# Attention and token mixer on one core: the max tiles in front of the loop made in pairs, with one VectorE maximum over two PSUM banks

## The chip, the cores and the metric

One Trainium2 chip, one of its cores. The metric is the device time of one execution in microseconds (us), less is better. Time before: 1671.52 us, median of 3 runs (1671.33 to 1672.03).

## What is computed

The output mixes two branches row by row with a gate, g = sigmoid(x . gate_w):

```python
q = (x @ wq) in 32 heads of 20;  k = x @ wk;  v = x @ wv      # one k and v for all heads
a = softmax(q k^T / sqrt(20)) v, heads joined, @ wo           # 2048 tokens x 2048 tokens, 32 times
u = gelu(layernorm(x)^T @ w1 + b1)                            # token axis: 640 x 1728
b = (u @ w2 + b2)^T                                           # 640 x 2048, turned back
out = g * a + (1 - g) * b                                     # 2048 x 640, float32
```

x is 2048 x 640. The softmax needs the maximum of every row of scores. The kernel makes it with scores of its own: a max matmul (the rows of q as weights, 512 columns of k as moving data) fills one PSUM bank, 128 queries by 512 keys, and VectorE reduces it to one column of 128 maxima. Four such columns, one for each block of 512 keys, belong to one row of scores.

## The kernel before, in words

The order of the work on each engine is written out by hand: every engine runs its instructions in the order in which the program issues them, and semaphores follow from which tiles they read and write. PSUM has 8 banks of 128 x 512 float32 here.

**Front (to 96.4 us).** x is turned and projected to q, k and v, q goes to a DRAM scratch (q_scr), LayerNorm fills h_hi and h_lo (x normalized, split into a high and a low part for float32 precision).

**The stage in front of the loop (96.4 to 168.2 us, lines 565 to 601).** It makes the first PRO = 8 of the 2 x 14 tiles of u. For each tile fc there are 16 steps (4 quarters hf by 4 chunks c); a step is six matmuls, three products (wh by h_hi, wh by h_lo, wl by h_hi), each on the two row halves of the array at once, into one PSUM bank per half (pu, psb: 2 x 2 banks). So there are 128 steps. Into them the program weaves two other things:

- *Leads* (lead, lines 569 to 572): max work for the loop, done ahead. After some steps, LEAD = 48 times in all, evenly spread from step 3 to step 122, a lead takes one max step of each row half b (ms_next, lines 467 to 487): one max matmul into one of the three banks of ps_m and one VectorE maximum over it (L482) into a column of mtiles. The two matmuls of a lead run on the two halves of the array.
- *Gelu steps* (gelu, lines 515 to 558): when a tile fc is done, ScalarE copies the first bank with the bias, and the further operations on VectorE, ScalarE and GpSimd (add, square, cube, tanh, product, high, low) are put on a list, one of which (or an empty place, None) is taken after each of the next steps (pop_chain). VectorE has two of them: add (L525), which reads the second bank, and cube (L529), which needs ScalarE's square of what add made.

ScalarE and GpSimd also split the next chunks of w1 into wh and wl (w1_upto). When 32 max steps of each half are done, ms_done reduces mtiles to the row maxima of unit 0 of 32 (L493), and store_max and fetch_max bring them to where the loop's score matmuls read them.

**The loop (from 168.2 us).** 326 turns; each weaves score matmuls (L657), exponentials (L660), products with v (L684), further max steps (L479, L482), and the products of the mixer's other tiles and of the output. Its max tiles alternate between ps_m and ps_s. The order of the max steps of a unit is given by ms_next's count k: the key block kq is the slowest, then the pair pr of heads, then the query block qt.

Banks in the stage: ps_m 3, ps_g 1 (used from the loop on), psb 4. Behind the stage psb is given up and ps_s (3) and ps_o (1) take its banks.

Of the kernel before, what the change touches and what calls it, by code (L numbers as in the profile page):

```python
# [9 lines left out]
F32 = mybir.dt.float32  # L10
F32R = mybir.dt.float32r
AF = mybir.ActivationFunctionType
ALU = mybir.AluOpType
AX = mybir.AxisListType
PSUM = bass.MemoryType.PSUM
DRAM = bass.MemoryType.DRAM

P = 128
# [6 lines left out]
NB = 512  # L25
NQB = S // NB
NQ = H // 4
NU = NQB * NQ
PRO = 8
LEAD = 48  # L30
# [9 lines left out]
def mix_kernel(ctx: ExitStack, tc: tile.TileContext, A_x, A_wq, A_wk, A_wv, A_wo,  # L40
               B_x, B_w1, B_b1, B_w2, B_b2, gate_w, out):
    nc = tc.nc
    x = A_x[0]
    y_out = out[0]

    def f32(ap):
        return ap.bitcast(F32)
# [11 lines left out]
    kst = const.tile([P, S], F32R, name="kst")  # L59
# [18 lines left out]
    right = ExitStack()  # L78
# [55 lines left out]
    def load_q(n, name):  # L134
        t = qp.tile([P, 2, NB], F32R, name=name)
        qb, g = divmod(n, NQ)
        cols = slice(qb * NB, (qb + 1) * NB)

        def part(b, j, src):
            o = 64 * b + DH * j  # L140
            rows = q_scr[src, g * 4 * DH:(g + 1) * 4 * DH, cols]
            nc.sync.dma_start(out=f32(t[o:o + DH]), in_=rows.rearrange("(a b d) q -> b d a q", a=2, b=2)[b])

        parts = [lambda b=b, j=j, src=src: part(b, j, src) for b in range(2) for j, src in enumerate((0, 1, 0))]
        if one_by_one[0]:
            q_parts_due.extend(parts)
        else:
            for f in parts:
                f()
        return t  # L150

    qtiles, qmax = {}, {}
    one_by_one, q_parts_due = [False], []

    def new_q(n):
        if n < NU:
            qtiles[n] = load_q(n, "qst")

    def new_qmax(n):
        if n < NU and n not in qmax:  # L160
            qmax[n] = load_q(n, "qmx")
# [285 lines left out]
    u_lo = [view(t, UC * HD2, UC) for t in (u0, slot[0])]  # L447
    pp_pool = ctx.enter_context(tc.tile_pool(name="pp", bufs=11))
    ev = ctx.enter_context(tc.tile_pool(name="ev", bufs=1))
    ps_m = ctx.enter_context(tc.tile_pool(name="ps_m", bufs=3, space=PSUM))  # L450
    ps_g = ctx.enter_context(tc.tile_pool(name="ps_g", bufs=1, space=PSUM))
    mpool = ctx.enter_context(tc.tile_pool(name="mpool", bufs=2))
    mmpool = ctx.enter_context(tc.tile_pool(name="mmpool", bufs=2))

# [1 line left out]
    mtiles = {}  # L456
    ring = []

    def next_bank():
        if not ring:  # L460
            return ps_m.tile([P, NB], F32, name="ms")
        ring[0] ^= 1
        return ps_m.tile([P, NB], F32, name="ms") if ring[0] else ps_s.tile([P, NB], F32, name="s")
    given = [0, 0]
    issued = [0, 0]

    def ms_next(b):
        k = given[b]
        if k >= 32 * NU:
            return None  # L470
        given[b] += 1
        n, r = divmod(k, 32)
        (kq, pr), qt = divmod(r // 4, 2), r % 4

        def step():
            if n not in mtiles:
                mtiles[n] = mpool.tile([P, 16, 4], F32, name="mp")
            ms = next_bank()
            nc.tensor.matmul(ms, qmax[n][64 * b:64 * b + 60, pr, qt * P:(qt + 1) * P],  # L479
                             kst[64 * b:64 * b + 60, kq * NB:(kq + 1) * NB], start=True, stop=True)  # L480
            c = (2 * b + pr) * 4 + qt
            nc.vector.tensor_reduce(mtiles[n][:, c, kq:kq + 1], ms, axis=AX.X, op=ALU.max)  # L482
            issued[b] += 1
            if min(issued) == 32 * n + 1:
                new_qmax(n + 1)

        return step

    def ms_done():
        n = len(row_max)  # L490
        if n < NU and min(issued) >= 32 * (n + 1):
            mm = mmpool.tile([P, 16], F32, name="mm")
            nc.vector.tensor_reduce(mm, mtiles.pop(n), axis=AX.X, op=ALU.max)  # L493
            mn = mmpool.tile([P, 2, 16], F32R, name="mn")
            nc.gpsimd.tensor_scalar(mm, mm, -1.0, None, op0=ALU.mult)
            nc.gpsimd.tensor_copy(mn[:, 0, :], mm)
            nc.gpsimd.tensor_sub(mn[:, 1, :], mm, f32(mn[:, 0, :]))
            row_max[n] = mn
# [14 lines left out]
    chain = []  # L513

    def gelu(d, fc, accs):
        both = fin.tile([P, D], F32, name="yo")
        xg, t1 = both[:, :HD2], both[:, HD2:]
        hi, lo = u_hi[d][:, fc, :], u_lo[d][:, fc, :]
        nc.scalar.activation(xg, accs[0][:, :HD2], AF.Identity, bias=bias[:, NS + fc:NS + fc + 1])

        def square():
            nc.scalar.activation(t1, xg, AF.Square)

        def add():
            nc.vector.tensor_add(xg, xg, accs[1][:, :HD2])  # L525
            square()

        def cube():
            nc.vector.scalar_tensor_tensor(t1, t1, 1.0 / 0.044715, xg, op0=ALU.add, op1=ALU.mult)  # L529

        def tanh():
            nc.scalar.activation(t1, t1, AF.Tanh, scale=GC * 0.044715)

        def high():
            nc.scalar.activation(hi, t1, AF.Copy)

        def low():
            nc.gpsimd.tensor_sub(lo, t1, f32(hi))

        def cube_p():  # L540
            nc.gpsimd.tensor_scalar(t1, t1, 1.0, 1.0 / 0.044715, op0=ALU.mult, op1=ALU.add)
            nc.gpsimd.tensor_mul(t1, t1, xg)

        def prod_p():
            nc.gpsimd.tensor_scalar(t1, t1, 1.0, 1.0, op0=ALU.mult, op1=ALU.add)
            nc.gpsimd.tensor_mul(t1, t1, xg)

        def high_p():
            nc.gpsimd.tensor_copy(hi, t1)
            nc.gpsimd.tensor_sub(lo, t1, f32(hi))  # L550

        if len(accs) == 2 and fc == PRO - 1:
            add()
            chain.extend((cube_p, None, tanh, prod_p, high_p))
        elif len(accs) == 2:
            chain.extend((None, None, add, None, cube, tanh, None, prod_p, None, None, None, high, None, low))
        else:
            chain.extend((square, cube_p, None, tanh, prod_p, high_p))

# [2 lines left out]
        if f:  # L562
            f()

    with tc.tile_pool(name="psb", bufs=2, space=PSUM, side="right") as psb:
        at, skip, last = 0, 3, NS * PRO - 6
        one_by_one[0] = True

        def lead():
            for b in range(2):  # L570
                ms_next(b)()
            ms_done()

        for fc in range(PRO):
            pu = [psb.tile([P, NB], F32, name=f"pu{r}") for r in range(2)]
            for hf in range(4):
                w1_upto(4 * fc + hf + 4)
                for f in [q_parts_due.pop(0) for _ in range(min(len(q_parts_due), 1 + fc // 5))] if fc else []:
                    f()
                wh, wl = w1t.pop(4 * fc + hf)  # L580
                for c in range(HS):
                    st = hf * HS + c
                    for k, (w, h) in enumerate(((wh, h_hi[0]), (wh, h_lo[0]), (wl, h_hi[0]))):
                        for r in range(2):
                            rows = slice(64 * r, 64 * r + 64)
                            nc.tensor.matmul(pu[r][:, :HD2], w[rows, c, :], h[rows, st, :],  # L586
                                             start=(st == 0 and k == 0), stop=(st == NS - 1 and k == 2))
                    done = [max(0, min(x, last) - skip) * LEAD // (last - skip) for x in (at, at + 1)]
                    if done[1] > done[0]:
                        lead()  # L590
                    at += 1
                    pop_chain()
                if fc == 1 and hf == 0:
                    new_q(0)
                if fc == PRO - 2 and hf == 2:
                    assert not q_parts_due
                    one_by_one[0] = False
                    fetch_max(0)
            gelu(0, fc, pu)
            if fc == PRO - 3:  # L600
                store_max(0)

    ps_s = ctx.enter_context(tc.tile_pool(name="ps_s", bufs=3, space=PSUM))
    ps_o = ctx.enter_context(tc.tile_pool(name="ps_o", bufs=1, space=PSUM))

# [26 lines left out]
    last = {"half": None, "ins": None, "sig": None}  # L632
# [331 lines left out]
    for st in range(NS):  # L964
        job = b2_jobs(st)
        if st < FIVE:
            for d in range(2):
                at = len(ph)
                ph += job[d]
        else:  # L970
            at = len(ph) + 6
# [87 lines left out]
    for k in range(len(ph)):  # L1059
        n = 0 if k == 0 else 1 + k % 2  # L1060
# [11 lines left out]
    for n in BLOCKS:  # L1072
# [3 lines left out]
        i = 0  # L1076
        while any(sc[b] < ends[b] for b in range(2)):
            b = int(sc[1] < sc[0])
# [6 lines left out]
        at = [0.0, 0.0]  # L1085
        while any(lanes) or any(fs):
            b = 0 if at[0] <= at[1] and (lanes[0] or fs[0]) or not (lanes[1] or fs[1]) else 1
# [18 lines left out]
    for c in range(CUT // P, DC):  # L1106
        r = min(P, HEAD - c * P)
        for st in held:
            oT, _ = room(len(jobs) - 4 + st - (NS - 4))
            for d in range(2):  # L1110
# [3 lines left out]
                for k, (j, w) in enumerate(((0, wo_hi), (1, wo_hi), (0, wo_lo))):  # L1114
                    nc.tensor.matmul(accs[st, d][:, :HD2], oT[:r, j, c, :], w[:r, c, d * HD2:(d + 1) * HD2],
                                     start=(k == 0 and c == CUT // P), stop=False)
# [5 lines left out]
    for i in range(4):  # L1122
        st = NS - 4 + i
        for d in range(2):
            at = pp_pool.tile([P, NB], F32, name="p")
# [3 lines left out]
            for k, (o, w) in enumerate(((oh, w_last[0]), (ol, w_last[0]), (oh, w_last[1]))):  # L1129
                nc.tensor.matmul(acc[:, :HD2], o[:, i * P:(i + 1) * P], w[:, sl],  # L1130
                                 start=(k == 0 and (st, d) not in accs), stop=(k == 2))
# [32 lines left out]
```

## Time and profile before

| | before |
|---|---|
| median of 3 runs | 1671.52 us |
| the profiled execution: device time | 1671.47 us |
| the profiled execution: span of its instructions | 1669.7 us |
| stage in front of the loop | 96.4 to 168.2 us, 71.8 us |
| TensorE / VectorE / ScalarE / GpSimd busy in the stage | 70.1 / 67.1 / 29.1 / 57.2 us |

How to read it: the span runs from the first instruction's start to the last one's end, and the device time has 1.8 us more around it. PE is TensorE's matmul, PEld its weight load (it runs beside the matmul before), DVE is VectorE, ACT ScalarE, POOL GpSimd, SP SyncE. L482 is line 482 of the kernel. A row of a group of instructions has line, engine, operation, output<-inputs, shapes and xcount, then the busy time in us and the mean of one in ns, then the engine's idle time just before them and who ended it. A row of waits names who waited for whom, in us, with the number of times and the longest. A row of the order of time has start, length, engine, line and operation; instructions of one kind behind each other are merged into one row with their count, and its length runs from the first start to the last end. A row of windows has the busy time of each engine in a stretch with the number of instructions, the clock granted to TensorE (1.00 is full), the DMA share and GB/s. Matmul ends are modelled.

### The profile page before, as it was taken

How to read it: one execution, taken by the hardware profiler on the slowest of the kernel's cores; microseconds unless marked ns; L12 is line 12 of the kernel's file. 1: busy time of each engine (PE TensorE's matmuls, PEld its weight loads, DVE VectorE, ACT ScalarE, POOL GpSimd, SP SyncE). 2: the span in 40 equal slices, each digit the busy share in tenths (PEclk: the TensorE clock that was granted, in tenths of full speed). 3: DMA queues.
4: the chain of work that ended last, by engine and by line, in shares of the span. 5: the costliest groups of instructions: out<-in, count | busy, mean ns of one | idle time of the engine just before them, and what ended most of it. 6: DMA issues, size and time to landing. Idle time of an engine off the chain costs nothing.

```text
span 1669.7 us, 38827 instructions
## 1 busy us (share of the span) xinstructions
PE 1661.0 (99%) x14865; PEld 1105.5 (66%) x14865; DVE 1435.7 (86%) x2732; ACT 1188.0 (71%) x2346; POOL 606.3 (36%) x759
## 2 busy tenths in 40 slices
PE   9999999999999999999999999999999999999998
PEld 7899666666666666666666666666666566666665
DVE  6689899999989999988888988988888998988933
ACT  4434777777777777777777777777777777777775
POOL 6578555455455554422232332122122220111210
PEclk9999999999999999999999999999999999999999
DMA  7665222222132232222222222212222121333611
GB/s 211 205 176 137 79 71 69 78 58 78 53 84 73 71 82 74 58 60 62 66 75 74 55 62 66 61 52 71 63 66 60 55 65 41 96 111 113 189 51 39
DMA packets 178305, 138.20 MB, mean 83 GB/s; under 512 B 33306, under 2 KB 144055, under 8 KB 178119
## 3 DMA queue, kind: packets, MB, share of 16 engines
q1 hardware_dynamic: 177830, 135.39, 28.9%
q8 instruction: 117, 1.92, 0.5%
q14 instruction: 70, 0.57, 0.1%
q10 hardware_dynamic: 288, 0.33, 0.1%
HBM read 102.36 MB, written 31.65 MB: 80 GB/s over the span
## 4 chain that ended last, share of the span: by engine, by line
PE 95%; issue 2%; DVE 1%; SPq 1%; ACT 0%; DMA 0%; POOL 0%; POOLq 0%; DVEq 0%; ACTq 0%
PE o L684 28%; PE ms L479 18%; PE s L657 13%; PE g L750 10%; PE g L929 7%; PE ms L657 5%; PE pp L298 4%; PE s L479 3%; PE pu L586 3%; PE g L875 2%; DVE mp L482 1%; PE ms L831 0%; ACT p L660 0%; PE pt L290 0%; SPq L195 0%
## 5 line engine op out<-in xcount | busy, mean ns | idle before, releaser
L482 DVE TENSOR_REDUCE mp<-ms 128x1 f32<-128x512 f32 x1514 | 967.2, 685 | 130.2 <-PE ms L479 102.7
L660 ACT ACTIVATE p<-s 128x512 f32<-128x512 f32 x1512 | 820.6, 606 | 299.4 <-PE s L657 280.2
L479 PE MATMUL ms<-kst,qmx 60*128 60x512 f32 x1514 | 646.5, 433 | 1.7 <-DVE mp L482 1.7
L657 PE MATMUL s<-qst,kst 62*128 62x512 f32 x1512 | 601.6, 403 | 0.0
L684 PE MATMUL o<-p,v_sb 128*32 128x512 f32 x4096 | 511.3, 601 | 0.0
L479 PEld LDWEIGHTS ms<-kst,qmx 60*128 60x128 f32 x1514 | 279.0, 184 | 244.9 <-ACT p L660 114.7
L482 DVE TENSOR_REDUCE mp<-s 128x1 f32<-128x512 f32 x534 | 355.6, 683 | 12.0 <-PE s L479 11.8
L660 ACT ACTIVATE p<-ms 128x512 f32<-128x512 f32 x536 | 305.1, 599 | 56.8 <-PE ms L657 50.2
L657 PEld LDWEIGHTS s<-qst,kst 62*128 62x128 f32 x1512 | 278.5, 186 | 55.2 <-DVE flag L670 31.0
L929 PE MATMUL g<-slot,wh 64*128 64x320 f32 x1280 | 297.5, 311 | 0.0
L129 POOL TENSOR_TENSOR wl<-wr,wh 128x512 fp32r<-128x512 f32 x176 | 228.6, 1300 | 43.8 <-PE g L750 17.3
L479 PE MATMUL s<-kst,qmx 60*128 60x512 f32 x534 | 230.8, 441 | 0.4 <-DVE yo L525 0.4
L684 PEld LDWEIGHTS o<-p,v_sb 128*32 128x32 f32 x4096 | 97.5, 108 | 185.3 <-issue 177.2
L657 PE MATMUL ms<-qst,kst 62*128 62x512 f32 x536 | 216.8, 405 | 0.0
L929 PEld LDWEIGHTS g<-slot,wh 64*128 64x128 f32 x1280 | 211.6, 184 | 2.0 <-issue 1.7
L750 PE MATMUL g<-slot,wh 64*128 64x320 f32 x864 | 202.1, 313 | 0.1
L750 PE MATMUL g<-u,wh 64*128 64x320 f32 x864 | 201.7, 312 | 0.0
L929 PE MATMUL g<-slot,wl 64*128 64x320 f32 x640 | 199.6, 312 | 0.0
L706 POOL TENSOR_TENSOR ot<-ot,rl 128x512 f32<-128x512 f32 x30 | 31.6, 1052 | 346.6 <-DVE rl L705 346.6
L128 POOL CAST wh<-wr 128x512 fp32r<-128x512 f32 x144 | 88.3, 613 | 188.0 <-PE g L750 81.5
L750 PEld LDWEIGHTS g<-slot,wh 64*128 64x128 f32 x864 | 143.5, 184 | 4.9 <-ACT yo L758 4.0
L750 PEld LDWEIGHTS g<-u,wh 64*128 64x128 f32 x864 | 143.5, 184 | 1.1 <-issue 1.1
(202 smaller groups left out, 2092.8 us busy)
## 6 DMA issues: line engine op xcount, KB each, us to landing
wr<-in_B_w_dram SPq DMA_DIRECT2D x152, 256.0 KB
qmx<-q_scr SPq DMA_DIRECT2D x192, 80.0 KB
qst<-q_scr SPq DMA_DIRECT2D x192, 80.0 KB
slot<-o_scr SPq DMA_DIRECT2D x20, 320.0 KB
y_scr<-yo SPq DMA_DIRECT2D x16, 320.0 KB
o_scr<-oh SPq DMA_DIRECT2D x124, 40.0 KB
o_scr<-ol SPq DMA_DIRECT2D x124, 40.0 KB
q_scr<-qh SPq DMA_DIRECT2D x19, 256.0 KB
```

The source lines that it names most:

```text
L128: nc.gpsimd.tensor_copy(wh, wr)
L129: nc.gpsimd.tensor_sub(wl, wr, f32(wh))
L298: nc.tensor.matmul(pp, w, t, start=first and n == 0, stop=not more and n == len(steps) - 1)
L479: nc.tensor.matmul(ms, qmax[n][64 * b:64 * b + 60, pr, qt * P:(qt + 1) * P], kst[64 * b:64 * b + 60, kq * NB:(kq + 1) * NB], start=True, s ...
L482: nc.vector.tensor_reduce(mtiles[n][:, c, kq:kq + 1], ms, axis=AX.X, op=ALU.max)
L586: nc.tensor.matmul(pu[r][:, :HD2], w[rows, c, :], h[rows, st, :], start=(st == 0 and k == 0), stop=(st == NS - 1 and k == 2))
L657: nc.tensor.matmul(s, kst[64 * b:64 * b + 62, kb * P:(kb + 1) * P], q[64 * b:64 * b + 62, pr, :], start=True, stop=True)
L660: nc.scalar.activation(p, s, AF.Exp, scale=SCALE)
L684: nc.tensor.matmul(o[32 * hh:32 * hh + 32, :], v_sb[:, kb, :], ptiles.pop((u, hh)), start=(kb == 0), stop=(kb == NS - 1), skip_group_check ...
L750: other_tile(half, nc.tensor.matmul(hold["p"][:, :HD2], w[r, fc % HS, :], u[d][r, fc, :], start=(hold["n"] == 1), stop=(hold["n"] == 6 * F ...
L875: other_tile(half, nc.tensor.matmul(hold["p"][:, :HD2], o[r, c, :], w[r, c, d * HD2:(d + 1) * HD2], start=(hold["n"] == 1), stop=(hold["n" ...
L929: other_tile(half, nc.tensor.matmul(hold["p"][:, :HD2], w[r, st % HS, :], h[d][r, st, :], start=(hold["n"] == 1), stop=(hold["n"] == 6 * NS)))
```

## The change

A lead in the stage now takes two max steps of each row half: four max matmuls into two double tiles (m2, two banks each, one for each half), in the order half 0, half 1, half 0, half 1, and then one VectorE maximum for each half over 2 x 512 columns, which writes two neighbouring columns of mtiles. There are 24 leads where there were 48, so the number of max matmuls in the stage stays 96, and that of maxima goes from 96 to 48. The two matmuls of a double tile have the same queries and the key blocks kq and kq + 1; so the count k is taken apart in another order, in the loop too: the lowest bit of kq is now the fastest. The pool of double tiles (psl, 2 x 2 banks) lives only in the stage; ps_m and ps_g are made behind it. In the list of gelu steps, cube, tanh and the product move back by one place each, and high and low stay where they were. The loop keeps its single banks and its maxima over 512.

```diff
-    ps_m = ctx.enter_context(tc.tile_pool(name="ps_m", bufs=3, space=PSUM))
-    ps_g = ctx.enter_context(tc.tile_pool(name="ps_g", bufs=1, space=PSUM))
...
     def next_bank():
-        if not ring:
-            return ps_m.tile([P, NB], F32, name="ms")
...
+    def ms_at(b):
+        k = given[b]
+        n, r = divmod(k, 32)
+        if n not in mtiles:
+            mtiles[n] = mpool.tile([P, 16, 4], F32, name="mp")
+        kq, pr, qt = 2 * (r // 16) + r % 2, r // 8 % 2, r // 2 % 4
+        return n, kq, pr, qt, (2 * b + pr) * 4 + qt
+
+    def ms_mm(ms, b, n, kq, pr, qt):
+        nc.tensor.matmul(ms, qmax[n][64 * b:64 * b + 60, pr, qt * P:(qt + 1) * P],
+                         kst[64 * b:64 * b + 60, kq * NB:(kq + 1) * NB], start=True, stop=True)
+
+    def ms_count(b, n, c):
+        issued[b] += c
+        if min(issued) > 32 * n:
+            new_qmax(n + 1)
...
-        (kq, pr), qt = divmod(r // 4, 2), r % 4
...
-            chain.extend((None, None, add, None, cube, tanh, None, prod_p, None, None, None, high, None, low))
+            chain.extend((None, None, add, None, None, cube, tanh, None, prod_p, None, None, high, None, low))
...
-    with tc.tile_pool(name="psb", bufs=2, space=PSUM, side="right") as psb:
+    with tc.tile_pool(name="psl", bufs=2, space=PSUM) as psl, \
+            tc.tile_pool(name="psb", bufs=2, space=PSUM, side="right") as psb:
...
         def lead():
-            for b in range(2):
-                ms_next(b)()
+            ats = [ms_at(b) for b in range(2)]
+            two = [psl.tile([P, 2, NB], F32, name="m2") for _ in range(2)]
+            for i in range(2):
+                for b, (n, kq, pr, qt, _) in enumerate(ats):
+                    ms_mm(two[b][:, i], b, n, kq + i, pr, qt)
+            for b, (n, kq, _, _, c) in enumerate(ats):
+                given[b] += 2
+                nc.vector.tensor_reduce(mtiles[n][:, c, kq:kq + 2], two[b], axis=AX.X, op=ALU.max)
+                ms_count(b, n, 2)
             ms_done()
...
-                    done = [max(0, min(x, last) - skip) * LEAD // (last - skip) for x in (at, at + 1)]
+                    done = [max(0, min(x, last) - skip) * (LEAD // 2) // (last - skip) for x in (at, at + 1)]
...
+    ps_m = ctx.enter_context(tc.tile_pool(name="ps_m", bufs=3, space=PSUM))
+    ps_g = ctx.enter_context(tc.tile_pool(name="ps_g", bufs=1, space=PSUM))
     ps_s = ctx.enter_context(tc.tile_pool(name="ps_s", bufs=3, space=PSUM))
```

More of the change, by code (lines that the diff above doesn't have):

```diff
@@ L465, in mix_kernel @@
     issued = [0, 0]
+    def ms_at(b):
[12 more added lines that the diff above has]
+            new_qmax(n + 1)
     def ms_next(b):
-        k = given[b]
-        if k >= 32 * NU:
+        if given[b] >= 32 * NU:
             return None
+        at = ms_at(b)
         given[b] += 1
-        n, r = divmod(k, 32)
-        (kq, pr), qt = divmod(r // 4, 2), r % 4
         def step():
-            if n not in mtiles:
-                mtiles[n] = mpool.tile([P, 16, 4], F32, name="mp")
+            n, kq, pr, qt, c = at
             ms = next_bank()
-            nc.tensor.matmul(ms, qmax[n][64 * b:64 * b + 60, pr, qt * P:(qt + 1) * P],
-                             kst[64 * b:64 * b + 60, kq * NB:(kq + 1) * NB], start=True, stop=True)
-            c = (2 * b + pr) * 4 + qt
+            ms_mm(ms, b, n, kq, pr, qt)
             nc.vector.tensor_reduce(mtiles[n][:, c, kq:kq + 1], ms, axis=AX.X, op=ALU.max)
-            issued[b] += 1
-            if min(issued) == 32 * n + 1:
-                new_qmax(n + 1)
+            ms_count(b, n, 1)
         return step
```

## The prediction

> **What bounds the kernel now.** I read the page first, then the busy times by stage, then the waits of TensorE, then VectorE's groups and the order of time inside the one stage that is edited. TensorE is the bound of the whole, and of the edited stage too, but there VectorE is close behind:
>
> ```profile
> span 1669.7 us, 38827 instructions
> PE 1661.0 (99%) x14865; PEld 1105.5 (66%) x14865; DVE 1435.7 (86%) x2732; ACT 1188.0 (71%) x2346; POOL 606.3 (36%) x759
> ```
>
> ```profile
> core 0: us, PE busy (x) PEld busy (x) DVE busy (x) ACT busy (x) POOL busy (x), PEclk, DMA share, GB/s
> ...
> 96.40:168.20 71.80, 70.08 (x866) 67.76 (x866) 67.10 (x119) 29.12 (x57) 57.19 (x58) 1.00 0.56 155
> 168.20:400.00 231.80, 231.39 (x2126) 151.29 (x2124) 207.88 (x394) 176.37 (x351) 118.93 (x155) 1.00 0.28 72
> ```
>
> The stage in front of the loop is the row 96.40 to 168.20: TensorE 70.1 and VectorE 67.1 of 71.8 us, at full clock. Behind it TensorE is busy 231.39 of 231.80 us, and from 168.3 us to the end its waits on other engines are these:
>
> ```profile
> PE s L479 <- DVE yo L525: 0.4, 1, 0.4
> PE g L831 <- DVE row L838: 0.2, 1, 0.2
> ```
>
> So nothing behind the stage can swallow a later start: what the stage loses or gains, the total loses or gains, one for one. Inside the stage, the max matmuls (L479) are the only TensorE work that waited, always for the maximum (L482):
>
> ```profile
> its engine sat idle before it (us, times) until:
>   DVE mp L482: 4.8, 9
> ```
>
> That view adds the weight loads to the matmuls, so 4.8 is not TensorE time; it says who is waited for. VectorE's work in the stage:
>
> ```profile
> L482 DVE TENSOR_REDUCE mp<-ms 128x1 f32<-128x512 f32 x96 | 59.7, 680 | 2.8 <-PE ms L479 1.8 <-PE pu L586 0.3
> L529 DVE SCALAR_TENSOR_TENSOR yo<-yo 128x320 f32<-128x320 f32 x7 | 3.6, 521 | 0.5 <-ACT yo L522 0.5
> ...
> L493 DVE TENSOR_REDUCE mm<-mp 128x16 f32<-128x64 f32 x1 | 0.2, 219 | 0.0
> ```
>
> **How fast TensorE could go.** From the order of time, TensorE only (start, length):
>
> ```profile
> 96.45 0.42 PE L586 MATMUL pu<-slot,wh 64*128 64x320 f32 x2
> ...
> 98.62 0.31 PE L586 MATMUL pu<-slot,wl 64*128 64x320 f32 x2
> ...
> 99.06 0.31 PE L586 MATMUL pu<-slot,wl 64*128 64x320 f32 x2
> 99.20 0.39 PE L479 MATMUL ms<-kst,qmx 60*128 60x512 f32 x2
> 99.44 0.46 PE L586 MATMUL pu<-slot,wh 64*128 64x320 f32 x4
> ...
> 150.26 0.39 PE L479 MATMUL ms<-kst,qmx 60*128 60x512 f32 x1
> ...
> 152.94 0.40 PE L479 MATMUL ms<-kst,qmx 60*128 60x512 f32 x1
> ...
> 168.23 0.30 PE L929 MATMUL g<-slot,wh 64*128 64x320 f32 x1
> ```
>
> A step (six matmuls, three pairs on the two row halves) holds one pair with wl: 98.62 to 99.06, so 0.44 us. A pair of max matmuls costs 99.44 - 99.20 = 0.24. From 150.26 to 152.94 there are two old leads and five steps without a wait: 2.68 us, which is just what a new lead (two pairs) and its five steps hold. The stage runs from 96.45 to the loop's first product at 168.23: 71.78 us.
>
> The new leads come after steps 8, 13, ..., 122: 23 gaps, 22 of five steps, one of four. With no wait at all the stage would take 99.20 - 96.45 + 2 x 0.44 = 3.63 up to the first lead, 22 x 2.68 + 2.24 = 61.20 between leads, and 2 x 0.24 + 6 x 0.44 = 3.12 from the last lead to the end: 67.95, **3.83 less** than now. That is the most that can be won.
>
> **The new wait.** Before, 48 leads of two banks ran round three banks, so a max matmul needed the maximum of three tiles earlier. Now a lead takes both double tiles, so that each tile is asked for again one lead later. TensorE's queue is in order: first matmul of half 0, first of half 1, second of half 0, second of half 1. The first of half 1 waits for half 1's maximum, the last thing VectorE does for the previous lead; the second of half 0 stands behind it, and without that one VectorE cannot start the next pair at all. That closes a ring, priced with these rows:
>
> ```profile
> 99.64 0.69 DVE L482 TENSOR_REDUCE mp<-ms 128x1 f32<-128x512 f32 x1 [0.92 <-PE ms L479]
> ...
> 109.38 6.30 DVE L482 TENSOR_REDUCE mp<-ms 128x1 f32<-128x512 f32 x10
> ...
> 153.91 0.68 DVE L482 TENSOR_REDUCE mp<-ms 128x1 f32<-128x512 f32 x1
> ```
>
> ```profile
> 154.65 0.49 PE L479 MATMUL ms<-kst,qmx 60*128 60x512 f32 x1 [0.20 <-DVE mp L482]
> 154.65 0.64 PE L586 MATMUL pu<-slot,wh 64*128 64x320 f32 x3
> ```
>
> - A max matmul that was waited for takes 0.49 instead of 0.39, and the next one on the other half starts with it (both rows say 154.65). I give 0.49 to the second of half 0.
> - From the end of that matmul to the maximum: 99.20 + 0.39 = 99.59 to 99.64, 0.05.
> - The maximum over 1024 is in no row. Length: 680 ns for 512 and 219 for 64 make 1.03 ns an element, and the 64 were in 16 groups, so groups are not dear; 0.68 + 0.53 = 1.21. Start to start, ten of 512 in 6.30 make (6.30 - 0.68) / 9 = 0.62, so the next starts 0.06 before the end: 1.21 - 0.06 = 1.15. Bounds: below, 1.05 for each (1024 elements with no fixed part); above, two maxima of now, 1.24 start to start and 1.30 long. I take 1.15 and 1.21, since the slope comes from the same instruction.
> - From its end to the waiting matmul: 153.91 + 0.68 = 154.59 to 154.65, 0.06.
>
> Ring: 0.49 + 0.05 + 1.15 + 1.21 + 0.06 = **2.96 us** a lead, against 2.68 of work. So TensorE waits about 0.28 at nearly every lead, where before it waited rarely. All that queues behind the waiting matmul are the products of the stage, the bound itself. 23 x 2.96 = 68.08.
>
> [...] The trace has 0.62 - 0.53 = 0.09 us of fixed part back to back, so 4.3 us, and all of it outside the ring.
>
> **Gelu steps.** VectorE has 2 x 1.15 = 2.30 to do in 2.96, so 0.66 is free between leads, and an add or a cube (below: cube at 108.98; the row of 109.38 above is the maximum behind it, so 0.40 start to start) fits in. In VectorE's order in the changed program, three of the seven cubes stand right behind their add, with no maximum between (before, two maxima or none). There VectorE waits for ScalarE's square:
>
> ```profile
> 108.98 0.48 DVE L529 SCALAR_TENSOR_TENSOR yo<-yo 128x320 f32<-128x320 f32 x1
> ...
> 161.01 0.68 DVE L482 TENSOR_REDUCE mp<-ms 128x1 f32<-128x512 f32 x1
> 161.61 0.48 DVE L525 TENSOR_TENSOR yo<-yo,pu 128x320 f32<-128x320 f32 x1
> 162.63 0.78 DVE L529 SCALAR_TENSOR_TENSOR yo<-yo 128x320 f32<-128x320 f32 x1 [0.54 <-ACT yo L522]
> 163.32 0.68 DVE L482 TENSOR_REDUCE mp<-ms 128x1 f32<-128x512 f32 x1
> ```
>
> Add to cube is 162.63 - 161.61 = 1.02, plus 0.40 for the cube, less the 0.66 that is free: 0.76 late, three times, 2.28. This one cube held the next maximum for 0.69 (163.32); with that it would be 1.05 each, but the seven cubes have a mean of 521 ns, so six of them were near 480 and I take the 0.40. The other moved steps run on ScalarE and GpSimd, 29 and 57 busy of 71.8, and cost nothing; ScalarE's and SyncE's orders are the same instruction for instruction.
>
> **At nothing.** The loop's orders are the same on every engine, with the same 512-column maxima; only which column block follows which differs, and matmuls, loads and maxima keep their number and shape. The two pools that are made later stand on the banks of the last lead: its second maximum ends 2.96 after the lead by the ring's terms, the loop's first product comes 3.12 after it, so that is hidden by 0.16; at the upper price of the maxima 0.02 would show. The one gap of four steps has less work, and the ring sets its length too.
>
> **Sum.** 3.63 + 68.08 + 2.28 + 3.12 = 77.11, against 71.78: **5.3 us slower**. The profiled execution took 1671.47 us (median of the runs 1671.52), so 1676.8.
>
> **Rivals.** (a) *No ring: the double banks keep VectorE fed and TensorE's present waits go.* Price: the 67.95 above, 1671.5 - 3.8 = 1667.7. It decides where the ring is under 2.68, that is where a maximum over both banks takes under 1.04 us. For it: fewer instructions on an engine that is busy 67.1 of 71.8. Against it: 512 elements take 0.68. 12%. [...] (b) *The ring is there, but near its floor*: maxima of 1.05 each make 0.49 + 0.05 + 1.05 + 1.05 + 0.06 = 2.70, 23 gaps 62.1, and with 2.28 and the ends 71.1: 1670.8, within 0.2%. It decides where both maxima show nothing but their elements. 18%. (c) *A maximum over two banks is no cheaper than two*: ring 0.49 + 0.05 + 1.24 + 1.30 + 0.06 = 3.14, 23 x 3.14 = 72.2, three late cubes at 1.05, 82.1 in all: 1681.8. 8%. The forecast itself, a ring between 2.86 and 3.05, has 62%.
>
> **How the numbers follow.** 0.2% of this time, 3.3 us, is about what a measurement can tell from no change. Slower by more than that: forecast and (c), 0.70; within it: (b), 0.18; faster: (a), 0.12. The range goes from 1671.8, which takes in the upper half of (b), to 1680.4, which leaves out most of (c); some 2 in 10 lie outside.
>
> **What would show it.** Right, if in the changed profile the double maximum takes about 1.21 us; if leads follow at about 2.96 us where their work is 2.68, TensorE waiting for the maximum at most of the 24; if three gaps are some 0.76 longer, each with a cube straight behind its add; if the stage takes about 77.1 us; and if the loop behind it keeps its length. Wrong, if max matmuls rarely wait (then (a) or (b)), or if the loop itself gets longer or shorter, which nothing here explains.

## The result, and the profile after

The changed kernel takes 1678.20 us (median, 1677.93 to 1678.62) against 1672.09 us for the kernel before measured with it: ratio 1.0037, 95% interval 1.0025 to 1.0048. It is 6.1 us slower. The forecast was 5.3 slower, 1676.8, range 1671.8 to 1680.4. The profiled execution took 1677.93 us.

Line numbers are those of the changed kernel from here on: L600 the stage's products, L472 the max matmul, L584 the double maximum (L583 in the runs with one tile for both halves), L525 ScalarE's read of a finished tile, L531 add, L535 cube, L551 and L552 the gelu product, L541 high (in e9 below L477 is the max matmul and L480 the maximum). The page of the changed kernel, and its busy times by stage (columns as in the rows of windows before):

```profile
span 1676.1 us, 38779 instructions
PE 1665.4 (99%) x14865; PEld 1104.6 (66%) x14865; DVE 1435.2 (86%) x2684; ACT 1187.2 (71%) x2346; POOL 604.4 (36%) x759
```

```profile
96.20:174.10 77.90, 74.53 (x865) 66.92 (x864) 65.97 (x71) 27.97 (x56) 54.17 (x56) 1.00 0.52 145
174.10:405.90 231.80, 231.14 (x2120) 150.83 (x2120) 207.92 (x394) 176.16 (x351) 119.49 (x156) 1.00 0.27 72
```

VectorE has 48 instructions less in the stage, and its busy time fell only from 67.1 to 66.0 us. The stage got longer, from TensorE's first product in it at 96.22 to the loop's first matmul:

```profile
96.22 0.42 PE L600 MATMUL pu<-slot,wh 64*128 64x320 f32 x2
...
99.85 0.62 PE L472 MATMUL m<-kst,qmx 60*128 60x512 f32 x4
...
115.04 0.39 PE L472 MATMUL m<-kst,qmx 60*128 60x512 f32 x1
...
115.45 0.73 PE L472 MATMUL m<-kst,qmx 60*128 60x512 f32 x3
...
118.40 0.50 PE L472 MATMUL m<-kst,qmx 60*128 60x512 f32 x2
...
174.79 0.49 PE L472 MATMUL ms<-kst,qmx 60*128 60x512 f32 x1 [0.42 <-DVE mp L584]
```

174.79 - 96.22 = 78.57 us against 71.78: **6.8 us more in the stage**. The front ended some 0.2 us earlier, and behind the stage the time is as long as before (the first product with v comes 6.51 us later than before, the last one 6.49), so the whole loss is in the stage, as the forecast had it. By the rows of windows TensorE's idle time in the stage rose only from 1.7 to 3.4 us, and its busy time from 70.1 to 74.5 with the same matmuls. A product's row lasts 0.30 us where the next matmul mostly starts 0.06 to 0.09 us later, so of the 0.33 us from 115.12 to 115.45, in which no matmul starts, only 0.03 counts as idle: most of the waiting is inside the busy time. Who was waited for, in the view of the max matmuls (the view that had 4.8 us, 9 times, before; the weight loads are in it again), and VectorE's groups:

```profile
its engine sat idle before it (us, times) until:
  DVE mp L584: 13.8, 30
```

```profile
L584 DVE TENSOR_REDUCE mp<-m 128x2 f32<-128x1024 f32 x48 | 56.5, 1218 | 10.1 <-PE m L472 10.1
L535 DVE SCALAR_TENSOR_TENSOR yo<-yo 128x320 f32<-128x320 f32 x7 | 5.5, 787 | 1.6 <-ACT yo L528 1.6
```

The double maximum takes 1218 ns. VectorE now waits 10.1 us for max matmuls (1.8 before), and TensorE waits for VectorE: the two engines take turns. VectorE in order of time:

```profile
108.68 0.47 DVE L531 TENSOR_TENSOR yo<-yo,pu 128x320 f32<-128x320 f32 x1
109.69 0.49 DVE L535 SCALAR_TENSOR_TENSOR yo<-yo 128x320 f32<-128x320 f32 x1 [0.54 <-ACT yo L528]
110.10 2.35 DVE L584 TENSOR_REDUCE mp<-m 128x2 f32<-128x1024 f32 x2
113.04 2.35 DVE L584 TENSOR_REDUCE mp<-m 128x2 f32<-128x1024 f32 x2 [0.59 <-PE m L472]
115.99 2.35 DVE L584 TENSOR_REDUCE mp<-m 128x2 f32<-128x1024 f32 x2 [0.60 <-PE m L472]
...
130.10 1.45 DVE L535 SCALAR_TENSOR_TENSOR yo<-yo 128x320 f32<-128x320 f32 x1
131.47 2.34 DVE L584 TENSOR_REDUCE mp<-m 128x2 f32<-128x1024 f32 x2
```

The ring can be read off: the waiting matmul starts at 115.45, the maxima at 115.99 (0.54 later), both end at 115.99 + 2.35 = 118.34, and at 118.40 the next lead's waiting matmul goes. That is 2.95 us, as in 18 of the 23 gaps (from one waiting matmul to the next), within 0.03.

The hold-up itself can be seen too. Half 0's maximum of the lead before ended at 113.04 + 1.22 = 114.26, and the first matmul of half 0 went at 115.04 without a wait. The second one of half 0 went only at 115.45, together with the first of half 1, which had waited for half 1's maximum to end at 113.04 + 2.35 = 115.39.

### The profile page after: what moved, and what is told of

Same layout as the page of the kernel before. It is cut to its first block, busy times and chain, and to the rows that moved or that the text cites. A ratio compares the mean times of both kernels' runs of the same rounds, so it can differ in the third digit from the quotient of the medians.

```text
span 1676.1 us, 38779 instructions
## 1 busy us (share of the span) xinstructions
PE 1665.4 (99%) x14865; PEld 1104.6 (66%) x14865; DVE 1435.2 (86%) x2684; ACT 1187.2 (71%) x2346; POOL 604.4 (36%) x759
## 4 chain that ended last, share of the span: by engine, by line
PE 93%; issue 3%; DVE 2%; SPq 1%; DMA 1%; POOL 1%; ACT 1%; POOLq 0%; DVEq 0%
PE o L700 28%; PE ms L472 17%; PE s L673 13%; PE g L766 10%; PE g L945 7%; PE ms L673 5%; PE pp L298 4%; PE s L472 3%; PE g L891 2%; PE pu L600 2%; DVE mp L584 1%; PE m L472 1%; PE ms L847 0%; ACT p L676 0%; DMA xa<-in_A_x_dram 0%
## 5 line engine op out<-in xcount | busy, mean ns | idle before, releaser
L490 DVE TENSOR_REDUCE mp<-ms 128x1 f32<-128x512 f32 x1418 | 907.7, 685 | 127.3 <-PE ms L472 100.6
L472 PE MATMUL ms<-kst,qmx 60*128 60x512 f32 x1418 | 615.6, 435 | 0.4 <-DVE mp L584 0.4
L472 PEld LDWEIGHTS ms<-kst,qmx 60*128 60x128 f32 x1418 | 261.7, 185 | 241.5 <-ACT p L676 114.5
L490 DVE TENSOR_REDUCE mp<-s 128x1 f32<-128x512 f32 x534 | 355.6, 683 | 12.0 <-PE s L472 11.7
L472 PE MATMUL s<-kst,qmx 60*128 60x512 f32 x534 | 230.8, 441 | 0.2 <-DVE yo L531 0.2
```

## The experiments

**The ring theory**: a lead takes both double tiles, so the wait for one half's maximum holds back the matmul that the other half's next maximum needs. **Rivals**: D, the double maximum itself is the loss, since it waits for two matmuls and holds two banks for 1.22 us; G, the new gelu places are the loss. The kernel before was run with each group (1671.57, 1671.60 and 1671.71 us). Stage is from the first product to the loop's first matmul, in the profiled execution; total is the median.

| run | what is in it | stage us | total us | ratio to before, 95% interval |
|---|---|---|---|---|
| before | 96 single maxima, 3 banks | 71.78 | 1671.5 to 1672.1 | |
| after | the change | 78.57 | 1678.20 | 1.0037 (1.0025 to 1.0048) |
| e1_cross | double tile from both halves | 69.70 | 1673.98 | 1.0015 (1.0006 to 1.0025) |
| e2_short_max | change, half-length maxima (half of the columns left out) | 68.46 | 1672.84 | 1.0008 (0.9998 to 1.0017) |
| e3_cube_late | change, cube 5 places behind add | 78.27 | 1678.05 | 1.0039 (1.0024 to 1.0054) |
| e4_four_single | before, 4 banks | 69.62 | 1669.51 | 0.9988 (0.9978 to 0.9997) |
| e5_late_psum | e3, cube reads PSUM (part of its factor left out) | 74.90 | 1674.78 | 1.0019 (1.0010 to 1.0029) |
| e6_cross_old | e1, gelu list of before | 69.15 | 1669.01 | 0.9985 (0.9976 to 0.9993) |
| e7_cross_old_act | e6, last casts on ScalarE | 68.39 | 1668.49 | 0.9982 (0.9973 to 0.9991) |
| e8_old_gelu | change, gelu list of before | 78.82 | 1678.79 | 1.0043 (1.0027 to 1.0059) |
| e9_four_act | e4, last casts on ScalarE | 68.81 | 1668.48 | 0.9979 (0.9970 to 0.9988) |

**e1_cross.** The same banks and the same 48 double maxima; only the matmuls that share a tile differ.

```diff
-            two = [psl.tile([P, 2, NB], F32, name="m2") for _ in range(2)]
-            for i in range(2):
-                for b, (n, kq, pr, qt, _) in enumerate(ats):
-                    ms_mm(two[b][:, i], b, n, kq + i, pr, qt)
+            two = psl.tile([P, 2, NB], F32, name="m2")
+            for b, (n, kq, pr, qt, _) in enumerate(ats):
+                ms_mm(two[:, b], b, n, kq, pr, qt)
+                given[b] += 1
...
+            nc.vector.tensor_reduce(mtiles[n][:, c:c + 9:8, kq], two, axis=AX.X, op=ALU.max)
...
-                    done = [max(0, min(x, last) - skip) * (LEAD // 2) // (last - skip) for x in (at, at + 1)]
+                    done = [max(0, min(x, last) - skip) * LEAD // (last - skip) for x in (at, at + 1)]
```

> The change, but a double tile holds one bank of each row half instead of two banks of one half: 48 leads again, each a pair of max matmuls into one double tile and one maximum over 1024 columns; two double tiles, used in turn. Same banks, same 48 maxima over 1024, same gelu places as the changed kernel. Ring theory (the loss comes from a lead that takes both double tiles, so that the wait of one tile's maximum holds back the matmul of the other): a tile is asked for two leads later, 2.68 us of TensorE work, and its maximum ends 0.39 + 0.05 + 1.22 after its lead, so TensorE hardly waits for maxima; what is left are some cubes behind late squares, 0.5 to 0.7 each, four or so: stage about 69.9 us against 78.6, total about 1670.4. Rival D (the double maximum itself is the loss: it waits for two matmuls and holds two banks for 1.22 us): nothing of that is changed, the stage stays near 78, total near 1678. Rival G (the gelu places are the loss): places are unchanged, near 1678 as well.

The stage took 69.70 us, where the ring theory had 69.9. D and G are out as the main cause, since they expected it to stay near 78. The total missed by 3.6 us, for a reason behind the stage. The fences show the waits of TensorE from 160 to 180 us, four stretches (the second is the wait, the third what follows), and GpSimd and ScalarE in order of time:

```profile
PE s L472 <- DVE yo L531: 4.0, 1, 4.0
```

```profile
160.00:166.00 6.00, 6.00 (x80) 5.88 (x76) 4.63 (x6) 1.59 (x4) 5.92 (x6) 1.00 0.47 133
166.00:170.20 4.20, 0.29 (x2) 0.03 (x1) 0.48 (x2) 0.89 (x2) 3.96 (x5) 0.76 0.47 125
170.20:175.00 4.80, 4.74 (x26) 4.70 (x28) 2.60 (x6) 3.26 (x7) 4.40 (x6) 0.50 0.52 132
175.00:180.00 5.00, 5.00 (x51) 3.29 (x50) 3.87 (x8) 3.68 (x8) 3.27 (x5) 1.00 0.58 163
```

```profile
166.08 1.26 POOL L129 TENSOR_TENSOR wl<-wr,wh 128x512 fp32r<-128x512 f32 x1
167.31 0.46 POOL L551 TENSOR_SCALAR yo<-yo 128x320 f32<-128x320 f32 x1
167.85 0.86 POOL L552 TENSOR_TENSOR yo<-yo 128x320 f32<-128x320 f32 x1
```

```profile
168.75 0.47 ACT L541 ACTIVATE u<-yo 128x320 fp32r<-128x320 f32 x1 [5.88 <-POOL yo L552]
169.12 0.51 ACT L525 ACTIVATE yo<-pu,bias 128x320 f32<-128x320 f32 x1
```

Tile 6's gelu product (L551, L552) stands in GpSimd's order behind two chunks of w1 and is done at 168.71; ScalarE's high (L541) waits for it, and behind that in ScalarE's order stands the read of the last tile's bank (L525), which the loop's first score bank needs. TensorE stood 4 us, and its granted clock was 0.76 in the mean of the second row and 0.50 in the third: 0.76 over 4.20 us is what 2.0 us at 0.50 make. So, if it fell in one step, an estimate, the clock was low some 1.9 us after the last matmul (166.29), and it stayed at 0.50 for the 4.8 us of work of the third row. From the loop's first matmul to the first product with v it took 11.7 us, in the kernel before 6.9.

**e2_short_max.**

```diff
-  nc.vector.tensor_reduce(mtiles[n][:, c, kq:kq + 2], two[b], axis=AX.X, op=ALU.max)
+  nc.vector.tensor_reduce(mtiles[n][:, c, kq:kq + 2], two[b][:, :, :NB // 2], axis=AX.X, op=ALU.max)
```

> The change, with each maximum over only the first 256 of the 512 columns of each bank: the maxima of the other columns in the stage are left out, so that a maximum takes about 0.68 us instead of 1.22; nothing else is changed. Ring theory: the ring is 0.49 + 0.05 + 0.61 + 0.68 + 0.06 = 1.89 us, under the 2.68 us of work between leads, so the waits for maxima vanish at all 23 gaps; the late cubes (1.0 us behind an add) now fit beside it: stage about 67.9, total about 1667.6. A rival in which four max matmuls at one place or the switch of the row halves cost TensorE the time by themselves: stage near 78, total near 1678.

```profile
  DVE mp L584: 0.4, 1
```

One wait for a maximum instead of 30 (the same view as in the result), stage 68.46 (67.9 expected), with the order of leads and matmuls unchanged. So the four matmuls at one place cost nothing that shows; the length of the maxima inside the ring does. The total is not told apart from before and missed 1667.6 by 5.2 us, again with the wait behind the stage:

```profile
PE s L472 <- DVE yo L531: 3.6, 1, 3.6
```

**e3_cube_late.**

```diff
-  chain.extend((None, None, add, None, None, cube, tanh, None, prod_p, None, None, high, None, low))
+  chain.extend((None, None, add, None, None, None, None, cube, tanh, None, prod_p, None, None, high, None, low))
```

> The change, with the cube five places behind the add instead of three (tanh, product, high and low move along): with a lead every five steps there is then always one lead between add and cube, so that no cube stands right behind its add. Ring theory: the three long gaps (3.69, 3.94 and 3.69 us instead of 2.95) go, and perhaps the two cubes that GpSimd held up (0.68 and about 0.6): 2.5 to 3.7 less, total 1674.5 to 1675.7, still 2.4 to 3.6 slower than before, with a wait for a maximum at each lead and gaps of 2.95. Rival G (gelu places are the loss): back to the time before, 1672, or under it.

Both theories expected more: no cube stands right behind its add now, and the stage got only 0.3 us shorter. The cube's group, and one cube beside GpSimd:

```profile
L535 DVE SCALAR_TENSOR_TENSOR yo<-yo 128x320 f32<-128x320 f32 x7 | 8.5, 1211 | 0.0
```

```profile
121.15 1.52 DVE L535 SCALAR_TENSOR_TENSOR yo<-yo 128x320 f32<-128x320 f32 x1
122.59 1.21 DVE L584 TENSOR_REDUCE mp<-m 128x2 f32<-128x1024 f32 x1
```

```profile
119.78 2.53 POOL L129 TENSOR_TENSOR wl<-wr,wh 128x512 fp32r<-128x512 f32 x2 [1.39 <-ACT wh L126]
```

Five of seven cubes took about 1.5 us instead of 0.48 (8.5 us for the seven). Each began while GpSimd ran a subtraction (here the pair ends at 119.78 + 2.53 = 122.31) and ended some 0.35 us after it. The long cube of the kernel before (162.63) and the two of the changed kernel (130.10 and 170.87) have the same 0.35. So the later place traded one hold-up for another.

**e5_late_psum** tests that, on e3's kernel.

```diff
-  nc.vector.scalar_tensor_tensor(t1, t1, 1.0 / 0.044715, xg, op0=ALU.add, op1=ALU.mult)
+  nc.vector.scalar_tensor_tensor(t1, t1, 1.0 / 0.044715, accs[1][:, :HD2], op0=ALU.add, op1=ALU.mult)
```

> The kernel of e3_cube_late with the cube's second factor read from the tile's second PSUM bank instead of from SBUF. This leaves part of the computation out: the cube's factor is the second half's sum alone, not the whole one. Theory of a shared way to SBUF: a cube with two SBUF operands cannot run while GpSimd's two-operand subtraction runs, and ends 0.35 us after it (so in all long cubes of the runs so far); with one operand in PSUM all seven cubes take about 0.48, the gaps of 3.7 us between leads go, only the ring's 2.95 is left: stage about 74.8 us against 78.3, total about 1674.5. Rival (the long cubes wait for ScalarE's square or for TensorE): no change, stage 78.3, total 1678.

```profile
L535 DVE SCALAR_TENSOR_TENSOR yo<-yo,pu 128x320 f32<-128x320 f32 x7 | 3.3, 478 | 0.0
```

```profile
  DVE mp L584: 7.6, 24
```

All seven cubes at 478 ns, stage 74.90 (74.8 expected), total 1674.78 (1674.5). Six of the seven began during a subtraction all the same. What is left is the ring alone, 24 short waits: 3.1 us over the stage of before, with no gelu delay in it. That is what the theory of the shared way expected: the long cubes, all with two SBUF inputs, ended 0.35 us after the subtraction that they began in, and with one input in PSUM the cube took its 478 ns. The runs show these times; that the two engines share a way to SBUF is the author's explanation of them.

**e8_old_gelu** undoes the second part of the change (the gelu list of before in the changed kernel; the diff is that of the change, turned round).

> The change with its second part undone: double tiles as in the changed kernel, gelu list of before. By the places of the leads, five cubes instead of three stand right behind their add; each costs about 0.75 us, and which cubes GpSimd holds up changes too (two did, about 0.7 each). Ring theory: gaps of 2.95 stay, total 1678 to 1680.5, 0 to 2 slower than the change. Rival G (the gelu places made the loss): back near 1672.

The total is 1678.79 and the stage 78.82, 0.25 more than with the change; the totals are not told apart, since the intervals of the two ratios overlap. All seven cubes took 0.48 to 0.49, but five instead of three stand behind their adds (gaps of 3.69 to 3.95). So the gelu part of the change is worth little, and G is out a second time.

**e4_four_single.** The kernel before, with ps_m and ps_g made behind the stage as in the change, and a pool of four single banks (lead_pool) for its leads:

```diff
-    ps_m = ctx.enter_context(tc.tile_pool(name="ps_m", bufs=3, space=PSUM))
-    ps_g = ctx.enter_context(tc.tile_pool(name="ps_g", bufs=1, space=PSUM))
...
         if not ring:
-            return ps_m.tile([P, NB], F32, name="ms")
+            return lead_pool[0].tile([P, NB], F32, name="ms")
...
+    with tc.tile_pool(name="psl", bufs=4, space=PSUM) as psl, \
```

> The kernel before with one part of the change alone: a fourth bank for the max tiles in the stage (the same four banks as in the change), single banks, 48 leads, maxima over 512, gelu places of before. Ring theory: no ring is made; with four banks round two per lead, a max matmul waits for the maximum of four tiles earlier instead of three, so the present waits of some 3.9 us in the stage fall by about half; VectorE's work (about 66 of the 71.8 us) is then the next limit: stage about 69.0 to 69.8, total 1669.4 to 1670.2. If the bank count does nothing: 1672.1.

The total is 1669.51 and the stage 69.62, both inside what was expected. The fourth bank by itself wins 2.1 us. Its stage still waits for maxima three times (2.4 us with the weight loads), in its last tile, where one cube was held up by GpSimd (1.29 us).

**e6_cross_old and e7_cross_old_act.** e1's tiles with the gelu list of before; then the casts of the four chunks that are split in the stage's last tile on ScalarE:

```diff
-            if c < 4 * PRO:
+            if c < 4 * PRO + 4:
                 nc.scalar.activation(wh, wr, AF.Copy)
```

> The kernel of e1_cross with the gelu list of before (cube four places behind, product one place earlier, so that the product stands ahead of the next chunk's cast and subtraction in GpSimd's order). Theory: the 4.0 us that TensorE waited behind e1_cross's stage came from GpSimd, whose order had the last product behind that chunk's split, and not from the tiles; with the list of before the wait is the 0.7 us of the kernel before again, and TensorE keeps its clock. Stage 67.8 to 68.8 us against 71.8 before, total 1667.5 to 1668.8, faster than both kernels. Rival (GpSimd's work as such, some 57 of 68 us, ends too late for a shorter stage): the wait behind the stage stays at 2 to 4 us with the half clock behind it, total 1671 to 1673.

> The kernel of e6_cross_old with the casts of the four chunks that are split during the stage's last tile on ScalarE instead of GpSimd, where all other casts of the stage are. If GpSimd still holds up the end of the stage in e6_cross_old: 0.5 to 2 us faster than it. If not: the same time within 0.4 us.

In e6 the wait behind the stage is 0.5 us, and the mean granted clock of its profiled execution is 0.999 (in e1 0.997); stage 69.15 and total 1669.01 are a little over what was expected. e7 takes 1668.49, 0.5 less. The stretch of e7's stage, all of TensorE's waits from its start to 175 us, and its maxima:

```profile
95.85:164.25 68.40, 68.06 (x867) 65.77 (x867) 63.50 (x71) 30.87 (x60) 54.98 (x55) 1.00 0.59 162
```

```profile
PE s L472 <- DVE yo L531: 0.5, 1, 0.5
PE m L472 <- DVE mp L583: 0.3, 1, 0.3
```

```profile
L583 DVE TENSOR_REDUCE mp<-m 128x2 f32<-128x1024 f32 x48 | 56.5, 1221 | 3.4 <-PE m L472 3.4
```

TensorE is busy 68.06 of 68.40 us: the 67.95 that the prediction gave as the least is nearly reached, with the double maximum and its four banks, and with the casts moved.

**e9_four_act**: e4 with e7's casts.

> The kernel of e4_four_single (four single banks, 96 maxima over 512) with the last tile's casts on ScalarE as in e7_cross_old_act, so that the two differ only in the maxima: 96 over one bank here, 48 over two banks there. If the maximum over two banks brings something by itself where it makes no ring: this one is slower than e7_cross_old_act by what VectorE's 4 us more of work cost TensorE, 0.5 to 1.2 us, total 1669.0 to 1669.7. If four banks and the casts are all that counts: the same, 1668.1 to 1668.9.

```profile
L480 DVE TENSOR_REDUCE mp<-ms 128x1 f32<-128x512 f32 x96 | 59.0, 679 | 1.5 <-PE ms L477 1.5
```

The total is 1668.48, the same as e7 (e9 ran on another chip, with a before of its own; the ratios agree too). VectorE has 2.5 us more maxima to do (59.0 against 56.5), and TensorE hardly sees it: the stage is 0.4 us longer in the profile. What won in both is the fourth bank and the casts taken off GpSimd; the double maximum brought nothing that shows in the total.

## Why the prediction was right

The direction, the mechanism and the size were right; the sum was short by 1.5 us in the stage.

- **The ring**: 2.96 forecast, 2.95 measured. e5, the ring without late cubes, has a stage of 74.90; the sum without its late cubes is 3.63 + 68.08 + 3.12 = 74.83. The ring's terms: 0.49 + 0.05 from the waiting matmul to the first maximum (0.54), 1.15 + 1.21 for the two maxima (2.35), 0.06 back. The maximum over 1024 took 1218 ns where 1.21 was derived from the rows for 512 and 64. e1 (other tiles, same maxima) and e2 (same tiles, shorter maxima) show that it needs both, a lead that takes both tiles and the long maximum.
- **Nothing behind the stage swallows it**: right for the change, the offset stays at 6.5 us to the end. Not right as a rule in the other direction: e1 and e2 show that a stage that is shorter by 2 to 3 us runs into GpSimd's order, which the prediction had left at nothing.
- **Late cubes**: three of 0.76 forecast; the gaps of 3.69, 3.94 and 3.69 us were 0.74, 0.99 and 0.74 over the ring. (The 3.94 has the reduction to row maxima in front of its add.)
- **The failed term**: a cube at 0.40 "with that it would be 1.05 each ... six of them were near 480 and I take the 0.40". The one long cube of the trace was not an oddity but a collision with GpSimd. The prediction also let GpSimd's moved steps "cost nothing". In the changed kernel two cubes met a subtraction: the gap at 130.10 was 3.63 (0.68 over the ring), and the one at 170.87 delayed the last maxima, so that the loop's first max matmul waited and the end took 174.79 - 171.01 = 3.78 instead of 3.12. In e5 and e8, where no cube was held up there, the end took 3.21 and 3.20, so 0.57 of it is that cube's. The two make 0.68 + 0.57 = 1.25 of the 1.46 us that were missing. The rest is small: the late cubes were 0.2 over their 2.28, the first gap (3.06) and the end 0.1 each, and 18 gaps of about 2.95 instead of 2.96 took some of it back.
- **The last lead hidden by 0.16**: as the terms stood, yes, and gone with that cube: 0.42 us of wait at 174.79.
- **Rivals**: (a) most of the win of up to 3.8 us exists, but not with this assignment of banks: e6 gets 2.6, and e7 and e9, which move casts too, get 3.1 and 3.2. (b) and (c) fell with the 1218 ns. One merge saved about 0.06 us of VectorE (1.22 for a double maximum, 1.28 for two single ones back to back), less than the 0.09 that the prediction took from the rows; its 4.3 us are that figure times 48, and the busy time of the maxima went from 59.7 to 56.5 us.

Open: no run gave out the four matmuls of a lead in another order (half 0, half 0, half 1, half 1) with the change's tiles and maxima. At 115.45 half 0's tile had been free for 1.2 us, so by the rows this order alone might loosen the ring. And the profiled loops of all nine experiments (from the first product with v to the last) were 0.3 to 0.5 us longer than those of before and after, while their stages began at 95.69 to 96.99; no run was made for either.

## What to carry to other kernels

Count buffers by when each is asked for again, not by number: four banks that one lead takes whole are no more than one buffer, and then producer and consumer take turns, with their latencies added to the period. Pair what is made at the same time (here the two row halves) into a tile, and give the next lead the other tile; four single banks did as well here. And before a stage is shortened, look at what the engines beside it still have in their queues at its end.

## What the runs showed of the hardware

- A VectorE scalar_tensor_tensor with two SBUF operands that began during a GpSimd subtraction of two 128x512 tiles ended about 0.35 us after it in every long case seen (up to 1.60 us instead of 0.48, at 170.87 in the changed kernel). The other way round, where cube and subtraction began within 0.02 us of each other, the cube took 0.48 and the subtraction about 1.65 us instead of 1.29 (six times in the kernel before). With one operand in PSUM the seven cubes took 478 ns in the mean (e5).
- A max matmul whose start was held up took 0.49 us instead of 0.39 (modelled ends), and so did the next one on the other, idle half (at 118.40 in the changed kernel the two ran for 0.50 us together).
- In a wait of 4.0 us without a matmul (e1) the granted clock was 0.76 in the mean of the 4.20 us around it and 0.50 in the 4.8 us of work behind it; one of 0.4 us in the kernel before (until 169.53) left it at 1.00, in the wait and in the 2.5 us behind it.
- One maximum over two PSUM banks took 1218 ns; two over one bank each, back to back, took 1.28 us (152.31 in the kernel before): merging saves about 0.06 us.
